# Attention backward: two passes over stored exponentials, or one pass with dS transposed by a DMA

## The chip, the cores and the metric

The kernel runs on one core of one Trainium2 chip. The metric is device time in microseconds (us) of one execution. The engines named below are PE (TensorE, matmuls), its weight loads (PEld), DVE (VectorE), ACT (ScalarE), POOL (GpSimd) and SP (SyncE, which only issues DMAs here).

## The reference

A transformer block, forward and backward (`jax.vjp`), with batch 1, S = 2048 tokens, D = 512, 32 heads of Dh = 16 columns and an MLP of F = 1792. The output and nine gradients are returned.

```python
def _A_ref(x, wqkv, wo):                       # H = 32, Dh = 16
    q, k, v = split heads of (x @ wqkv)
    scores = jnp.einsum('bhqd,bhkd->bhqk', q, k) * Dh ** (-0.5)
    p = _softmax(scores, axis=-1)
    o = jnp.einsum('bhqk,bhkd->bhqd', p, v)
    return merge heads of (o) @ wo
def _B_ref(x, w1, b1, w2, b2):
    r = relu(x @ w1 + b1)
    return (r * r) @ w2 + b2
mod = silu(c) @ w_mod          # sa, ca, ga, sb, cb, gb
x = x + ga * _A_ref(_layernorm(x) * (1 + ca) + sa, A_wqkv, A_wo)
x = x + gb * _B_ref(_layernorm(x) * (1 + cb) + sb, B_w1, B_b1, B_w2, B_b2)
_out, _vjp = jax.vjp(_f, ...); return (_out, *_vjp(grad_out))
```

For each head the attention backward needs P = exp(scale QK^T) (2048 x 2048), dP = dO V^T, dS = P * dP, and then dQ = dS K, dK = dS^T Q and dV = P^T dO. The 1/rowsum and the row term of the softmax gradient are folded into extra columns of the padded dO and V operands, so that dS is one product of two tiles.

## The kernel before

The work is cut in phases, which run one after the other: forward projections and attention (`phase12`), output projection and MLP forward (`phase3`), MLP backward and the gradient into the attention (`phase4`), attention backward (`phase5`), and the gradients of wqkv, wo and the modulation (`phase6`). Instructions are written in program order; a tile framework then sets buffers, semaphores and, by its own costs, some small moves in the order of each engine. Each engine executes its list in order.

**Units.** Attention is done for pairs of heads. For each of the 16 pairs (`pidx`, that is group `g` of four heads and half `jp`), each of four blocks of 512 columns (`c0`) and each of 16 blocks of 128 rows (`ib`) there is one unit: 1024 units in a pass. Heads are 16 columns wide, padded to 32 rows, so four heads fill the 128 rows of a transposed operand (`QTq_d`, `KTq_d`, `VTq_d`, `dOTq_d` in DRAM). A matmul over all 128 rows would mix the four heads, so one operand is a masked tile with zeros in the rows of the other three (`make_masked`, `load_masked`, L446 and L457).

**Forward** (L409 to L418): two score matmuls of 512 columns per unit, one exp of 1024 columns (ACT), eight matmuls of 17 columns with 128x128 pieces of `pu` as weights. With `self.stash` each `pu` is also stored to DRAM (`put_d`, L415, 256 KB per unit). The pool of `pu` has 8 buffers with `stash` and 3 without it.

**Pass A** (`attn_bwd_pass("A")`) makes dQ, with keys on the partitions. It loads `pu` back from `put_d` (L1185, on SP), makes dP with two matmuls of 512 columns (L1201), copies two of three dP tiles from PSUM with ACT (L1144), multiplies on DVE (L1145 from the copy, L1147 straight from PSUM), and adds eight matmuls of 16 columns into dQ (L1116). In it runs, as a background generator stepped every few units, the gradient of the MLP weights (`gen_4b_bg`, L805 to L885): 14 blocks of 128 MLP columns.

**Pass B** (`attn_bwd_pass("B")`) makes dK and dV, with queries on the partitions. Per unit it makes scores (L1190, two matmuls of 512 columns into `st`) and dP (L1193, two into `dp`), exp of the scores again (L1197, two of 512 columns), the product on DVE (L1147) and, two units late (`LAG`), sixteen matmuls of 16 columns: eight with `ds` as weights (L1120, dK), eight with `pu` as weights (L1123, dV). `st` has three PSUM buffers of one bank, `dp` two of two banks. At its start the loads for phase 6 (`wq_6`, `dx1b_6`, L1064 and L1065) are issued on POOL.

Of the kernel before, what the change touches and what calls it, by code (L numbers as in the profile page):

```python
# [33 lines left out]
class K:  # L34
# [29 lines left out]
    def build(self, ctx: ExitStack):  # L64
# [21 lines left out]
        self.stash = self.opts.get("stash", True)  # L86
# [963 lines left out]
    def phase45(self):  # L1050
        pass

    def phase5(self):
        tc, nc, pp, io = self.tc, self.nc, self.pp, self.io
        S, D, H, NQ, ST, DT = self.S, self.D, self.H, self.NQ, self.ST, self.DT
# [4 lines left out]
        self.dk_t = opb.tile([P, ST, D], BF16, name="dk_t")  # L1060
        self.dv_t = opb.tile([P, ST, D], BF16, name="dv_t")
# [6 lines left out]
    def attn_bwd_pass(self, mode, bg=None):  # L1068
        tc, nc = self.tc, self.nc
        S, D, H, NQ, ST = self.S, self.D, self.H, self.NQ, self.ST  # L1070
        loadA = (mode == "A" and self.stash)
        exp_split = self.opts.get("exp_split", False)
        LAG = self.opts.get("lagA", 3) if loadA else 2
        act_frac = self.opts.get("act_frac", (2, 3))
        with ExitStack() as es:
            cp = es.enter_context(tc.tile_pool(name=f"p5{mode}c", bufs=1))
            qp = es.enter_context(tc.tile_pool(name=f"p5{mode}q", bufs=2))
            sb = es.enter_context(tc.tile_pool(name=f"p5{mode}s", bufs=LAG + 2))
            bg_gen, bg_n = (None, 0)
            if bg is not None:  # L1080
                bg_gen, bg_n = bg(es)
            if loadA:
                ldp = es.enter_context(tc.tile_pool(name=f"p5{mode}ld", bufs=self.opts.get("ld_bufs", 15)))
                tmpp = es.enter_context(tc.tile_pool(name=f"p5{mode}tmp", bufs=3))
                dpp = es.enter_context(tc.tile_pool(name=f"p5{mode}dp", bufs=3, space=PSUM))
            else:
                stp = es.enter_context(tc.tile_pool(name=f"p5{mode}st", bufs=3, space=PSUM))
                dpp = es.enter_context(tc.tile_pool(name=f"p5{mode}dp", bufs=2, space=PSUM))
            accp = es.enter_context(tc.tile_pool(name=f"p5{mode}acc", bufs=1, space=PSUM))
            if mode == "A":  # L1090
                Ktm = cp.tile([P, ST, D], BF16, name="Ktm")
                nc.sync.dma_start(Ktm[:], self.ktm_d.rearrange("(st p) d -> p st d", p=P))
            else:
                Qtm = cp.tile([P, ST, D], BF16, name="Qtm")
                nc.sync.dma_start(Qtm[:], self.qtm_d.rearrange("(st p) d -> p st d", p=P))
                dOp = cp.tile([P, ST, D], BF16, name="dOp")
                nc.gpsimd.dma_start(dOp[:], self.dOp_d.rearrange("(st p) d -> p st d", p=P))
            accbank = accp.tile([P, 2, 256], F32, name="accbank")
            accbank4 = accbank[:].rearrange("p a (b c) -> p (a b) c", b=2)
            nacc = 128 if mode == "A" else 256  # L1100
            pend = []
            state = {"grp": 0, "u": 0}
            units_total = 2 * NQ * self.SC * ST
            bg_every = max(1, (units_total * 9 // 10) // max(1, bg_n))

            def stage4(u):
                (g, jp, c0, cw, ib, nib, heads, rows, acc, pu, ds) = u
                nsub = cw // P
                if ib == 0:
                    nc.vector.memset(acc[:, :nacc], 0.0)  # L1110
                for a in range(2):
                    h = heads[a]
                    for sub in range(nsub):
                        if mode == "A":
                            o = acc[:, (a * 4 + sub) * DH:(a * 4 + sub + 1) * DH]
                            nc.tensor.matmul(o, lhsT=ds[:, a, sub * P:(sub + 1) * P], rhs=Ktm[:, ib, h * DH:(h + 1) * DH],  # L1116
                                             start=False, stop=False, skip_group_check=True)
                        else:
                            o = acc[:, (a * 4 + sub) * DH:(a * 4 + sub + 1) * DH]
                            nc.tensor.matmul(o, lhsT=ds[:, a, sub * P:(sub + 1) * P], rhs=Qtm[:, ib, h * DH:(h + 1) * DH],  # L1120
                                             start=False, stop=False, skip_group_check=True)
                            o2 = acc[:, 128 + (a * 4 + sub) * DH:128 + (a * 4 + sub + 1) * DH]
                            nc.tensor.matmul(o2, lhsT=pu[:, a, sub * P:(sub + 1) * P], rhs=dOp[:, ib, h * DH:(h + 1) * DH],  # L1123
                                             start=False, stop=False, skip_group_check=True)
                if ib == nib - 1:
                    st0 = c0 // P
                    h0 = heads[0]
                    if mode == "A":
                        dst = self.dq_t[:, st0:st0 + nsub, h0 * DH:(h0 + 2) * DH].rearrange("p s (a d) -> p a s d", a=2)
                        src = acc[:, 0:128].rearrange("p (a s d) -> p a s d", a=2, s=4)[:, :, :nsub, :]  # L1130
                        nc.vector.tensor_scalar(dst, src, self.scale, None, ALU.mult)
                    else:
                        dst = self.dk_t[:, st0:st0 + nsub, h0 * DH:(h0 + 2) * DH].rearrange("p s (a d) -> p a s d", a=2)
                        src = acc[:, 0:128].rearrange("p (a s d) -> p a s d", a=2, s=4)[:, :, :nsub, :]
                        nc.vector.tensor_scalar(dst, src, self.scale, None, ALU.mult)
                        dst = self.dv_t[:, st0:st0 + nsub, h0 * DH:(h0 + 2) * DH].rearrange("p s (a d) -> p a s d", a=2)
                        src = acc[:, 128:256].rearrange("p (a s d) -> p a s d", a=2, s=4)[:, :, :nsub, :]
                        nc.scalar.copy(dst, src)

            def consumer(dp, pu, cw):  # L1140
                ds = sb.tile([P, 2, 512], BF16, name="ds")
# [337 lines left out]
```

The softmax here doesn't subtract the row's maximum and nothing guards it: scores larger than these inputs give would overflow.

## Time and profile before

| what | value |
|---|---|
| runs of the kernel | 3949.59 and 3952.64 us, median 3951.11 |
| span of the profiled execution | 3955.1 us |
| busy share PE / DVE / ACT / POOL | 87% / 68% / 77% / 8% |
| DMA | 727.01 MB, mean 184 GB/s |
| PE from / to: pass A (L1201, L1116) | 1474.8 to 2434.0 us |
| PE from / to: pass B (L1193, L1123) | 2439.8 to 3782.7 us |
| phase 6 (first matmul L1235) | from 3796.1 us |

The runs shown were taken without the profiler. The profiled execution is known by its span alone, 4 us (0.1%) above their median; sums in this text are made against 3955.1 and then lowered by 4. In the profile a share of busy time is an average over phases with different limits, so the phases are read one by one. A matmul's record lasts until its result is written; the next one starts earlier than that, so the distance between two starts is what a matmul costs when they follow each other.

### The profile page before, as it was taken

What the parts mean: (1) busy time and instruction counts of PE and PEld (TensorE: products, weight loads), DVE (VectorE), ACT (ScalarE), POOL (GpSimd) and SP (SyncE); (2) the same over time, 40 slices, a digit from 0 to 9 for tenths busy, and PEclk for the clock granted to TensorE, in tenths of its full rate; (3) what the DMA queues carried; (4) which work ended last, traced back from release to release, by engine and by line L of the source; (5) the groups of instructions that cost most, each with busy time, mean ns of one, the idle gap of its engine ahead of it and who ended that gap; (6) DMA issues with size and microseconds to landing.
All of it is one profiled execution on the core that took longest, in us unless ns stands there. A gap on an engine that the chain in (4) does not pass through costs nothing. (4 is left out here: it accounts for less than half of the span.)

```text
span 3955.1 us, 109981 instructions
## 1 busy us (share of the span) xinstructions
PE 3447.8 (87%) x44824; PEld 1950.4 (49%) x45590; DVE 2683.9 (68%) x3839; ACT 3053.2 (77%) x4423; POOL 334.0 (8%) x428
## 2 busy tenths in 40 slices
PE   5999988888686848888888878999999999999987
PEld 2555533333233325555555544666666666666643
DVE  6222210000244649999999998999999999999965
ACT  3999999999532438888888767888888888888843
POOL 3111100000100340111111110000000000000000
PEclk8999999999898969999999999999999999999998
DMA  3999988887724679999999897000000000000032
GB/s 123 333 333 336 332 309 292 298 297 289 263 91 163 212 190 332 322 320 337 321 322 329 289 323 231 9 18 9 19 20 8 19 9 18 19 9 6 2 125 74
DMA packets 414007, 727.01 MB, mean 184 GB/s; under 512 B 52697, under 2 KB 121050, under 8 KB 413498
## 3 DMA queue, kind: packets, MB, share of 16 engines
q1 hardware_dynamic: 381114, 630.90, 45.9%
q0 software_dynamic: 23760, 79.32, 5.9%
q10 hardware_dynamic: 8624, 9.70, 0.8%
q8 instruction: 356, 5.83, 0.6%
q14 instruction: 153, 1.25, 0.1%
HBM read 383.65 MB, written 336.07 MB: 182 GB/s over the span
## 5 line engine op out<-in xcount | busy, mean ns | idle before, releaser
L1147 DVE TENSOR_TENSOR ds<-dp,pu 128x1024 bf16<-128x1024 f32 x1365 | 1658.4, 1220 | 71.6 <-ACT pu L1197 24.0
L1197 ACT ACTIVATE pu<-st 128x512 bf16<-128x512 f32 x2048 | 1112.6, 597 | 229.9 <-PE st L1190 167.2
L412 ACT ACTIVATE pu<-st 128x1024 bf16<-128x1024 f32 x1024 | 938.8, 1621 | 0.0
L1144 ACT CAST dpb<-dp 128x1024 bf16<-128x1024 f32 x683 | 666.3, 1026 | 180.5 <-PE dp L1201 149.1
L1201 PE MATMUL dp<-dOTm,VTq 128*128 128x512 bf16 x1853 | 567.0, 382 | 96.7 <-ACT dpb L1144 78.2
L1190 PE MATMUL st<-KTm,QTq 128*128 128x512 bf16 x2047 | 628.0, 378 | 23.9 <-ACT pu L1197 16.6
L409 PE MATMUL st<-QTm,KTq 128*128 128x512 bf16 x1856 | 564.8, 377 | 9.6 <-ACT pu L412 4.4
L1120 PEld LDWEIGHTS <-ds 128*128 128x128 bf16 x8192 | 499.6, 96 | 115.0 <-DVE ds L1147 0.9
L1193 PE MATMUL dp<-VTm,dOTq 128*128 128x512 bf16 x1729 | 540.0, 379 | 5.5 <-DMA KTm<-KTq_d 5.5
L1120 PE MATMUL accbank<-Qtm,ds 128*128 128x16 bf16 x8192 | 529.1, 170 | 17.4 <-DVE ds L1147 0.7
L1123 PE MATMUL accbank<-dOp,pu 128*128 128x16 bf16 x8192 | 525.7, 169 | 0.0
L1123 PEld LDWEIGHTS <-pu 128*128 128x128 bf16 x8192 | 458.1, 96 | 113.6 <-issue 0.3
L1145 DVE TENSOR_TENSOR ds<-dpb,pu 128x1024 bf16<-128x1024 bf16 x683 | 472.8, 708 | 58.0 <-ACT dpb L1144 54.5
L418 PEld LDWEIGHTS <-pu 128*128 128x128 bf16 x8192 | 293.5, 96 | 443.3 <-ACT pu L412 381.2
L1116 PEld LDWEIGHTS <-ds 128*128 128x128 bf16 x8192 | 318.5, 96 | 247.5 <-DVE ds L1145 59.1
L418 PE MATMUL accbank<-Vaug,pu 128*128 128x17 bf16 x8192 | 352.3, 172 | 91.2 <-ACT pu L412 41.1
L427 DVE RECIPROCAL rl<-accbank 128x4 f32<-128x4 f32 x128 | 22.9, 179 | 527.4 <-PE accbank L418 527.3
L1116 PE MATMUL accbank<-Ktm,ds 128*128 128x16 bf16 x8192 | 336.7, 170 | 21.8 <-DVE ds L1145 6.0
L1193 PEld LDWEIGHTS <-dOTq 128*128 128x128 bf16 x2048 | 196.8, 96 | 287.0 <-DVE ds L1147 34.6
L1201 PEld LDWEIGHTS <-VTq 128*128 128x128 bf16 x2048 | 159.9, 96 | 162.2 <-issue 116.7
L288 DVE TENSOR_SCALAR ev_fm<-pps,bcol 128x512 bf16<-128x512 f32 x92 | 69.1, 751 | 186.4 <-PE pps L281 184.3
L409 PEld LDWEIGHTS <-KTq 128*128 128x128 bf16 x2048 | 130.4, 96 | 40.9 <-issue 24.2
(308 smaller groups left out, 2676.5 us busy)
## 6 DMA issues: line engine op xcount, KB each, us to landing
put_d<-pu SPq DMA_DIRECT2D x1024, 256.0 KB
pu<-put_d SPq DMA_DIRECT2D x1024, 256.0 KB
rT_d<-rT SPq DMA_DIRECT2D x4, 1792.0 KB
rT<-rT_d SPq DMA_DIRECT2D x4, 1792.0 KB
duT_d<-duT POOLq DMA_DIRECT2D x4, 1792.0 KB, 12.8
rT_f<-rT_d POOLq DMA_DIRECT2D x14, 512.0 KB, 6.6
duT_f<-duT_d POOLq DMA_DIRECT2D x14, 512.0 KB, 7.2
xhat_d<-xhat SPq DMA_DIRECT2D x2, 2048.0 KB
```

The source lines that it names most:

```text
L409: nc.tensor.matmul(stt[:, a, :qw], lhsT=KT[:, kb * P:(kb + 1) * P], rhs=QTm[a][:, q0:q0 + qw], start=True, stop=True)
L412: nc.scalar.activation(pu[:, :, :qw], stt[:, :, :qw], ACT.Exp, scale=self.scale)
L418: nc.tensor.matmul(acc[:, a, sub, :], lhsT=pu[:, a, sub * P:(sub + 1) * P], rhs=Vaug[:, kb, heads[a], :], start=False, stop=False, skip_gr ...
L1116: nc.tensor.matmul(o, lhsT=ds[:, a, sub * P:(sub + 1) * P], rhs=Ktm[:, ib, h * DH:(h + 1) * DH], start=False, stop=False, skip_group_check ...
L1120: nc.tensor.matmul(o, lhsT=ds[:, a, sub * P:(sub + 1) * P], rhs=Qtm[:, ib, h * DH:(h + 1) * DH], start=False, stop=False, skip_group_check ...
L1123: nc.tensor.matmul(o2, lhsT=pu[:, a, sub * P:(sub + 1) * P], rhs=dOp[:, ib, h * DH:(h + 1) * DH], start=False, stop=False, skip_group_chec ...
L1144: nc.scalar.copy(tmp[:, :, :cw], dp[:, :, :cw])
L1147: nc.vector.tensor_tensor(ds[:, :, :cw], dp[:, :, :cw], pu[:, :, :cw], ALU.mult)
L1190: nc.tensor.matmul(sts[a][:, :cw], lhsT=L1[:, ib * P:(ib + 1) * P], rhs=R1[a][:, c0:c0 + cw], start=True, stop=True)
L1193: nc.tensor.matmul(dp[:, a, :cw], lhsT=L2[:, ib * P:(ib + 1) * P], rhs=R2[a][:, c0:c0 + cw], start=True, stop=True)
L1197: nc.scalar.activation(pu[:, a, :cw], sts[a][:, :cw], ACT.Exp, scale=self.scale)
L1201: nc.tensor.matmul(dp[:, a, :cw], lhsT=L2[:, ib * P:(ib + 1) * P], rhs=R2[a][:, c0:c0 + cw], start=True, stop=True)
```

## The change

`self.stash` is set to False: the forward pass stores no `pu`, and its pool has 3 buffers. The MLP weight gradients leave the background of pass A and run by themselves before the attention backward (`phase45`, with `gen_4b` in place of `gen_4b_bg`). The two passes become one, `attn_bwd`, with queries on the partitions as in pass B. Its score and dP matmuls take 32 rows of both operands, without masked tiles. dK and dV are made as in pass B (`kv`, two units late). For dQ, the `ds` tiles of two units, 128 x 2048 values or 512 KB, are transposed in sixteen 128x128 blocks by one DMA on SP's queue (`dma_start_transpose`, L1177), and three pairs late (`LAGQ`) sixteen matmuls of 16 columns with the transposed blocks as weights add into dQ (`dq`, L1137). `st` has two PSUM buffers, one for each head. All loads of operands go through POOL's queue, one group of four heads ahead; the loads for phase 6 come after the pass. The lines that the diff removes are those of `phase5` and `attn_bwd_pass` above.

```diff
-        self.stash = self.opts.get("stash", True)
+        self.stash = False
...
     def phase45(self):
-        pass
+        with tc.tile_pool(name="p4b", bufs=1) as sb2, tc.tile_pool(name="p4bl", bufs=2) as lb, \
+                tc.tile_pool(name="p4bo", bufs=2) as ob, \
+                tc.tile_pool(name="p4bacc", bufs=1, space=PSUM) as accps, \
+                tc.tile_pool(name="p4bps", bufs=2, space=PSUM) as ps, \
+                tc.tile_pool(name="p4btr", bufs=1, space=PSUM) as trps:
+            for _ in self.gen_4b(sb2, lb, ob, accps, ps, trps):
+                pass
     def phase5(self):
-        self.attn_bwd_pass("A", bg=self.bg_4b)
+        self.attn_bwd()
         opb = self.open_pool("p56b", bufs=1)
...
         nc.gpsimd.dma_start(self.wq_6[:], io["A_wqkv"].rearrange("(kt p) n -> p kt n", p=P))
         nc.gpsimd.dma_start(self.dx1b_6[:], self.dx1b_d.rearrange("(st p) d -> p st d", p=P))
-        self.attn_bwd_pass("B")
...
+    def attn_bwd(self):
+        LAG, LAGQ = 2, 3
+        W = 4 * DH
+            qp = es.enter_context(tc.tile_pool(name="p5q", bufs=2))
+            pup = es.enter_context(tc.tile_pool(name="p5pu", bufs=LAG + 3))
+            dsp = es.enter_context(tc.tile_pool(name="p5ds", bufs=5))
+            dtp = es.enter_context(tc.tile_pool(name="p5dt", bufs=LAGQ + 2))
+            stp = es.enter_context(tc.tile_pool(name="p5st", bufs=2, space=PSUM))
+            dpp = es.enter_context(tc.tile_pool(name="p5dp", bufs=2, space=PSUM))
+            accp = es.enter_context(tc.tile_pool(name="p5acc", bufs=1, space=PSUM))
+            acckv = accp.tile([P, 2, 2, 2, 4, DH], F32, name="acckv")
+            accq = accp.tile([P, ST, 2, DH], F32, name="accq")
...
+            def kv(u):
...
+                    for sub in range(4):
+                        nc.tensor.matmul(acc[:, 0, a, sub, :], lhsT=ds[:, a, sub * P:(sub + 1) * P],
+                                         rhs=T["Q"][:, ib, col:col + DH], start=False, stop=False, skip_group_check=True)
+                        nc.tensor.matmul(acc[:, 1, a, sub, :], lhsT=pu[:, a, sub * P:(sub + 1) * P],
+                                         rhs=T["dO"][:, ib, col:col + DH], start=False, stop=False, skip_group_check=True)
...
+            def dq(u):
...
+                for i in range(2):
+                    for a in range(2):
+                        for sub in range(4):
+                            nc.tensor.matmul(accq[:, ib0 + i, a, :], lhsT=dsT[:, (i * 2 + a) * 4 + sub, :],
+                                             rhs=T["K"][:, 4 * c + sub, col:col + DH], start=False, stop=False,
+                                             skip_group_check=True)
...
+                        for ib0 in range(0, ST, 2):
+                            ds2 = dsp.tile([P, 2, 2, 512], BF16, name="ds")
+                            for i in range(2):
+                                sts = [stp.tile([P, 512], F32, name="st") for a in range(2)]
+                                dp = dpp.tile([P, 2, 512], F32, name="dp")
+                                for a in range(2):
+                                    r = 32 * (2 * jp + a)
+                                    nc.tensor.matmul(sts[a][:], lhsT=T["QT"][r:r + 32, q], rhs=T["KT"][r:r + 32, c0:c0 + 512],
+                                                     start=True, stop=True)
+                                for a in range(2):
+                                    r = 32 * ((2 * jp + a + 2) % 4)
+                                    nc.tensor.matmul(dp[:, a, :], lhsT=T["dOT"][r:r + 32, q], rhs=T["VT"][r:r + 32, c0:c0 + 512],
+                                                     start=True, stop=True)
+                                pu = pup.tile([P, 2, 512], BF16, name="pu")
+                                for a in range(2):
+                                    nc.scalar.activation(pu[:, a, :], sts[a][:], ACT.Exp, scale=self.scale)
+                                if len(pend) >= LAG:
+                                    kv(pend.pop(0))
+                                nc.vector.tensor_tensor(ds2[:, i], dp[:], pu[:], ALU.mult)
+                                pend.append((T, g, jp, c, ib, acc, pu, ds2[:, i]))
+                            dsT = dtp.tile([P, 16, P], BF16, name="dsT")
+                            nc.sync.dma_start_transpose(dsT[:], ds2[:].rearrange("p i a k -> p (i a k)"))
+                            if len(pendq) >= LAGQ:
+                                dq(pendq.pop(0))
+                            pendq.append((T, g, jp, c, ib0, dsT))
```

What `gen_4b` does for each of its 14 blocks `ft` (line numbers of the kernel after the change):

```python
nc.scalar.activation(aT_f[:], rT_f[:], ACT.Square)
for (srcT, dst, eng) in ((aT_f, a_blk, "act"), (duT_f, du_blk, "dve")):
    for s0 in range(0, ST, 8):                        # two groups of eight
        pt = trps.tile([P, 8 * P], BF16, name="trps") # one PSUM buffer
        ...                                           # 8 transposes (L717), one copy out by eng
g2 = ...   # 16 matmuls of 512 columns (L725), then two DVE products and an f32 matmul (L731)
g4 = ...   # 64 matmuls of 128 columns (L736), an f32 matmul (L741), six DVE operations
```

**One unit on PE, before (pass B).** `st` and `dp` are the tiles of scores and dP, `KTm` and `VTm` the masked operands; each large matmul covers 128 rows.

```order
L1190 LDWEIGHTS QTq_60875
L1190 MATMUL st_61797<-KTm0_39029,QTq_60875 128x512
L1190 LDWEIGHTS QTq_60875
L1190 MATMUL st_61798<-KTm1_39031,QTq_60875 128x512
L1193 LDWEIGHTS dOTq_60877
L1193 MATMUL dp_61771<-VTm0_39037,dOTq_60877 128x512
L1193 LDWEIGHTS dOTq_60877
L1193 MATMUL dp_61771<-VTm1_39039,dOTq_60877 128x512
L1120 LDWEIGHTS ds_61739
L1120 MATMUL accbank_39028<-Qtm_39024,ds_61739 128x16
L1123 LDWEIGHTS pu_61720
L1123 MATMUL accbank_39028<-dOp_39026,pu_61720 128x16
```

The same place in PE's list after the change, with the end of a `dq` (`dsT` is the transposed tile, `Kg` the group's K):

```order
L1137 LDWEIGHTS dsT_28071
L1137 MATMUL accq_20930<-Kg_20953,dsT_28071 128x16
L1163 LDWEIGHTS QTq_20945
L1163 MATMUL st_28311<-KTq_20947,QTq_20945 128x512
L1163 LDWEIGHTS QTq_20945
L1163 MATMUL st_28312<-KTq_20947,QTq_20945 128x512
L1137 LDWEIGHTS dsT_28144
L1137 MATMUL accq_20930<-Kg_20953,dsT_28144 128x16
```

The four large matmuls stay; they now take unmasked operands at 32 rows each, and the small matmuls of `dq` stand in the same list, here even between `st` and `dp`. In most units (878 of 1024) the four stand together; PE's list goes from one kind of matmul to the other 2449 times in all.

**SP's queue, before (pass A).** The loads of stored exponentials alternate with those of masked operands.

```order
L457 DMA dOTm_19712<-dOTq_d 32x512
L1185 DMA pu<-put_d 128x1024 x3
L457 DMA dOTm_19714<-dOTq_d 32x512
L1185 DMA pu<-put_d 128x1024 x12
L457 DMA dOTm_19712<-dOTq_d 32x512
```

After the change SP has the transposes alone between the stores of `gen_4b` (L728, L751) and the first DMAs of phase 6:

```order
L728 DMA out_dram<-dw_20763 128x512
L751 DMA out_dram<-dw_20843 128x4x128
L1177 DMA_TRANSPOSE dsT<-ds 128x16x128 x512
L1365 DMA out_dram<-dwm_59021 128x4x512
L1199 DMA O_tm<-O_d 128x16x512
```

The 1024 loads of 256 KB, and in the forward pass as many stores, have left; 512 transposes of 512 KB have come, and whatever follows them on SP starts after the last of them is issued.

More of the change, by code (lines that the diff above doesn't have):

```diff
@@ L1109, in stage4 @@
                 if ib == 0:
-                    nc.vector.memset(acc[:, :nacc], 0.0)
+                    nc.vector.memset(acc, 0.0)
                 for a in range(2):
[L1112 to L1138, printed above, removed]
@@ new lines, in kv @@
+                    col = (2 * jp + a) * DH
+                    for sub in range(4):
[3 more added lines that the diff above has]
+                                         rhs=T["dO"][:, ib, col:col + DH], start=False, stop=False, skip_group_check=True)
@@ new lines, in attn_bwd @@
+            T = load_group(0)
+            n = 0
+            for g in range(NQ):
+                Tn = load_group(g + 1) if g + 1 < NQ else None
+                for jp in range(2):
+                    for c in range(SC):
+                        c0 = 512 * c
+                        acc = acckv[:, n % 2]
+                        n += 1
+                        for ib0 in range(0, ST, 2):
+                            ds2 = dsp.tile([P, 2, 2, 512], BF16, name="ds")
+                            for i in range(2):
+                                ib = ib0 + i
+                                q = slice(ib * P, (ib + 1) * P)
+                                sts = [stp.tile([P, 512], F32, name="st") for a in range(2)]
[20 more added lines that the diff above has]
+                            pendq.append((T, g, jp, c, ib0, dsT))
+                T = Tn
@@ L1210, in attn_bwd_pass @@
             while pend:
-                stage4(pend.pop(0))
-            if bg_gen is not None:
-                for _ in bg_gen:
-                    pass
+                kv(pend.pop(0))
+            while pendq:
+                dq(pendq.pop(0))
     def phase6(self):
```

147 lines of the change are left out of this document (36 added, 111 removed).

## The prediction

> **What bounds the kernel now.** I read the page's first line, then the busy time of each engine in five stretches cut where the phases begin (forward; MLP and preparation; pass A; pass B; phase 6), because one share for the whole span mixes stages with different limits.
>
> ```profile
> span 3955.1 us, 109981 instructions
> ```
>
> ```profile
> core 0: us, PE busy (x) PEld busy (x) DVE busy (x) ACT busy (x) POOL busy (x), PEclk, DMA share, GB/s
> 90.00:1050.00 960.00, 836.53 (x10574) 404.86 (x10768) 157.35 (x504) 942.76 (x1027) 66.87 (x122) 0.99 0.85 311
> 1050.00:1474.00 424.00, 291.90 (x1541) 139.82 (x1569) 207.07 (x475) 143.36 (x282) 97.96 (x118) 0.84 0.52 165
> 1474.00:2436.00 962.00, 835.30 (x11612) 511.69 (x11818) 893.15 (x1229) 762.55 (x869) 130.85 (x140) 0.98 0.93 317
> 2436.00:3786.00 1350.00, 1304.88 (x20175) 810.40 (x20497) 1271.53 (x1157) 1115.51 (x2112) 6.55 (x11) 1.00 0.06 17
> 3786.00:3956.00 170.00, 132.11 (x724) 62.77 (x736) 96.71 (x266) 60.64 (x99) 3.16 (x5) 0.90 0.35 112
> ```
>
> The forward stretch is ACT's (942.76 of 960). Pass A has DVE (893) and DMA (0.93) both near their end; pass B has PE (1305) and DVE (1272) near theirs, with almost no DMA. The change replaces 962 + 1350 = 2312 us by one pass and a foreground phase. Which engine is really full in pass B is seen in its timeline, one unit of it:
>
> ```profile
> 3000.34 0.59 PE L1190 MATMUL st<-KTm,QTq 128*128 128x512 bf16 x2
> 3000.76 1.08 ACT L1197 ACTIVATE pu<-st 128x512 bf16<-128x512 f32 x2 [0.18 <-PE st L1190]
> 3000.78 0.59 PE L1193 MATMUL dp<-VTm,dOTq 128*128 128x512 bf16 x2
> ...
> 3001.20 0.17 PE L1120 MATMUL accbank<-Qtm,ds 128*128 128x16 bf16 x1
> ...
> 3001.23 0.17 PE L1123 MATMUL accbank<-dOp,pu 128*128 128x16 bf16 x1
> ...
> 3001.59 0.17 PE L1123 MATMUL accbank<-dOp,pu 128*128 128x16 bf16 x1
> ...
> 3001.61 0.59 PE L1190 MATMUL st<-KTm,QTq 128*128 128x512 bf16 x2
> ```
>
> From one unit's first score matmul to the next is 3001.61 - 3000.34 = 1.27 us without a hole: four large matmuls at (3001.20 - 3000.34)/4 = 0.216, sixteen small ones at (3001.61 - 3001.20)/16 = 0.0255. PE bounds pass B, ACT waits for it, and DVE is close behind, as its group and the wait show (mean ns of one before the last bar):
>
> ```profile
> L1147 DVE TENSOR_TENSOR ds<-dp,pu 128x1024 bf16<-128x1024 f32 x1365 | 1658.4, 1220 | 71.6 <-ACT pu L1197 24.0
> L1197 ACT ACTIVATE pu<-st 128x512 bf16<-128x512 f32 x2048 | 1112.6, 597 | 229.9 <-PE st L1190 167.2
> L1190 PE MATMUL st<-KTm,QTq 128*128 128x512 bf16 x2047 | 628.0, 378 | 23.9 <-ACT pu L1197 16.6
> L1120 PE MATMUL accbank<-Qtm,ds 128*128 128x16 bf16 x8192 | 529.1, 170 | 17.4 <-DVE ds L1147 0.7
> ```
>
> ```profile
> ACT pu L1197 <- PE st L1190: 137.2, 683, 0.5
> ```
>
> **The new pass.** Per unit DVE keeps its 1.22 us and ACT its 2 x 0.597 = 1.19. PE gets 24 small matmuls in place of 16 (0.61 us). The four large ones are unknown twice over. They use four different sets of 32 rows, so they may run side by side: from 0.216 apart (as now) down to nothing; I take a quarter, 0.054. And where the list passes from small to large matmuls PE may have to finish what it holds: 0.170 - 0.025 = 0.15 behind a small one and 0.378 - 0.216 = 0.16 behind a large one by the records' lengths, or nothing. I take both in full, as the careful end: an overlap of two shapes is in no row. What these two choices are worth depends on a loop, since `st` has one buffer per head where it had three in common. From the end of a unit's second exp: 0.04 until PE takes the next unit's second score matmul (3000.76 lies 0.04 after the first one's 0.38), then dP, dP at 0.054 each and 0.38 to the end of the last: 0.53; 16 `kv` at 0.0255 and, in every other unit, 16 `dq`: 0.82; finish, 0.15; the following unit's first score, 0.38 + 0.04; its two exps, 1.19. That is 3.11 us, in which two units pass: 512 x 3.11 = 1592. I take **1590**. With no price for the passing the large ones need 0.04 + 3 x 0.054 before `kv`, and the loop is 0.20 + 0.82 + 0.42 + 1.19 = 2.63 (DVE alone 2.44): 512 x 2.63 = 1347, and with the 64 column ends, at which `acckv` is cleared and written out by DVE, about 1390, the lower bound.
>
> ```profile
> L1135 DVE TENSOR_SCALAR dk_t<-accbank 128x128 bf16<-128x128 f32 x64 | 18.6, 291 | 10.5 <-PE accbank L1123 10.4
> L1138 ACT CAST dv_t<-accbank 128x128 bf16<-128x128 f32 x64 | 16.7, 260 | 3.0 <-DVE dk_t L1135 3.0
> L1110 DVE MEMSET accbank<- 128x256 f32 x53 | 14.4, 272 | 2.7
> ```
>
> (64 x (0.29 + 0.26 + 0.27) = 52 us.) With nothing side by side and both prices, PE alone needs per two units 8 x 0.216 + 48 x 0.0255 + 2 x 0.31 = 3.57: 1828, the upper bound.
>
> [...]
>
> **The transposes.** No row shows one. 512 of them, of 512 KB, must each be through the queue in 3.11 us to be hidden. `dq` comes three pairs late, so latency is covered by about two pairs, 6 us; the rate counts. From below, pass A's plain loads, 317 GB/s at a DMA share of 0.93: 524288 B / 317 = 1.65 us. From above, if each 256-byte piece (one row of a 128x128 block, 2048 in a transpose) takes a packet as ACT's queue shows them, 0.008 x 16 x 3955.1 / 8624 = 59 ns, over 16 engines: 7.5 us.
>
> ```profile
> q10 hardware_dynamic: 8624, 9.70, 0.8%
> ...
> pu<-put_d SPq DMA_DIRECT2D x1024, 256.0 KB
> ...
> dOTq<-dOTq_d POOLq DMA_DIRECT2D x8, 512.0 KB, 5.1
> ...
> dx1b<-dx1b_d POOLq DMA_DIRECT2D x1, 2048.0 KB, 19.2
> ...
> wqkv<-in_A_wqkv_dram POOLq DMA_DIRECT2D x1, 1536.0 KB, 10.2
> ```
>
> I take 1.65: same queue, nearly the same rows per partition (2 KB there, 4 KB here), and at the time of the pass hardly any other DMA. At that, nothing of it is on the path. If it isn't so, the weight load of L1137 waits on PE, behind it stand the next units' scores, and ACT and DVE run dry.
>
> [...]
>
> **The MLP gradients in the foreground.** Rows of the background version and of an f32 matmul:
>
> ```profile
> 1979.97 0.61 PE L834 MATMUL gps<-ident,rT_f 128*128 128x128 bf16 x8
> ```
>
> ```profile
> 1967.35 1.11 PE L851 MATMUL gps<-du_blk,xh 128*128 128x128 bf16 x17
> ```
>
> ```profile
> 1478.25 1.56 PE L808 MATMUL gps<-g2w,ones_f 128*128 128x512 f32 x2
> ```
>
> ```profile
> L835 ACT COPY a_blk<-gps 128x1024 bf16<-128x1024 bf16 x28 | 28.8, 1028 | 1.1 <-PE gps L834 1.0
> L826 ACT ACTIVATE rT_f<-rT_f 128x2048 bf16<-128x2048 bf16 x14 | 27.3, 1948 | 0.0
> ```
>
> A 128-column matmul costs (1.11 - 0.22)/16 = 0.056 us (0.22 is one record's length). Per block PE has (32 + 64) x 0.056 + 16 x 0.216 + about 1.0 in f32 = 9.9 us. One PSUM buffer takes all four groups of transposes, so two ACT copies (1.03) and part of the DVE copies stand in the way: about 2.6 more, 12.5 us, times 14 = 175, and 15 for the start and the closing sums: **190**. Bounds: 140 (PE alone, 14 x 9.9) and 240 (copies and the square, 1.95, all in line: 14 x 17).
>
> **The rest.** The first group's seven loads are at the pass's start (5.1 us for one of 512 KB): 20, from 5 to 40. The last transpose and `dq`: 8, from 4 to 12. Phase 6's loads come late now (19.2 us to landing), where pass B covered them: 10, from 0 to 20. The masked loads had cover already. In the forward pass the stores go, which leaves ACT's chain as it is:
>
> ```profile
> L412 ACT ACTIVATE pu<-st 128x1024 bf16<-128x1024 f32 x1024 | 938.8, 1621 | 0.0
> ```
>
> ACT has no idle time ahead of this exp: 0. Either sign is possible: up to 17 us gained (960 - 943), or as much lost if three `pu` buffers hold up the exp; its cover is that PE uses `pu` at once.
>
> **Sum**, on the profiled span: 1474 + 190 + 20 + 1590 + 8 + 10 + 170 = 3462. The span is 4 above the median of the runs: **3460**, 12% less than before.
>
> **Rivals.**
> - *The shapes mix freely* (pass 1390): 3262 - 4 = 3258. For it: the rows are disjoint. Against: list order and the one `st` buffer per head.
> - *The transposes set the pace, below break-even.* A transpose of 3.6 us, the middle between 3.1 and 4.07, makes the pass 512 x 3.6 = 1843 and the time 3711. For it: one queue issues all, in order, and no row shows how fast it issues pieces of this kind. Against: 3.1 us is only 524288 B / 3.1 us = 169 GB/s, where plain loads made 317. [...]
> - *The transposes are slow, and the kernel is slower than before.* The other terms sum to 1872, so it decides from (3955 - 1872)/512 = 4.07 us on. At 5.0 us the pass is 2560 and the time 4428; at the upper bound of 7.5, 5708. For it: if the transpose goes in pieces of 256 bytes at the pace of the packet row, it takes 7.5. Against: the source rows are 4 KB long, and pass B's DMA share of 0.06 says that the engines are free.
> - *The change doesn't do what it says*: the 32-row matmuls follow one another, with both prices. Pass 1828, time 3696; still faster, and in the forecast's own range.
>
> **How the numbers follow.** Forecast 0.44 (own range 3340 to 3700, with the 240 of the foreground's end), free mixing 0.12, pace below break-even 0.15, slow transposes 0.29. The kernel's runs can tell 2% from no change: faster means below 3872, slower above 4030. Faster is 0.44 + 0.12 + 0.15 less 0.02 near the edge: 0.69; within 2% 0.04; slower 0.27. The range starts at 3220 (free mixing with a cheap foreground, 0.02 left out) and reaches to 4450, transposes of 5.0 us; beyond that I leave 0.17.
>
> **What would show it.** In the changed kernel's profile: distance between units in the middle of the pass (1.55 forecast; 1.3 for free mixing); starts of the four large matmuls (0.05 or 0.22 apart); idle PE before the first small one. If the transposes set the pace, PE's weight load of L1137 waits for a DMA and the pass is 512 times the distance of two transposes. The foreground should lie between 1474 and some 1665. The forecast is wrong first of all if a transpose takes over 3.1 us.

## The result and the profile after

| what | before | after |
|---|---|---|
| median of the runs | 3951.11 us | 3645.28 us (3640.79 to 3649.78) |
| span of the profiled execution | 3955.1 us | 3638.7 us |
| attention backward (first to last PE instruction) | 1474.8 to 3782.7 | 1644.2 to 3463.7 |
| mean granted PE clock | 0.97 | 0.72 |

The time falls to 0.9226 of before (0.9198 to 0.9254): 7.7% less, where 12% was forecast. The first rows of the page and of its picture of the span:

```profile
span 3638.7 us, 99498 instructions
...
PEclk8999999999989897995555555555555555555588
DMA  3111100000032555639999999999999999999952
```

The clock row reads 5 from slice 19 to slice 38 of 40: over the new pass, and in no other slice, PE is granted half its clock. The stretches, cut as before (forward; MLP and preparation; the foreground of MLP gradients; the pass; phase 6):

```profile
core 0: us, PE busy (x) PEld busy (x) DVE busy (x) ACT busy (x) POOL busy (x), PEclk, DMA share, GB/s
90.00:1050.00 960.00, 840.84 (x10564) 400.45 (x10762) 157.14 (x501) 942.18 (x1026) 65.71 (x119) 0.99 0.09 29
1050.00:1460.00 410.00, 286.34 (x1525) 137.59 (x1551) 197.45 (x479) 143.11 (x281) 84.78 (x105) 0.85 0.50 161
1460.00:1643.00 183.00, 154.43 (x1625) 108.57 (x1640) 96.14 (x182) 58.59 (x57) 17.74 (x32) 0.97 0.46 145
1643.00:3466.00 1823.00, 1675.89 (x28679) 954.96 (x28681) 1309.12 (x1252) 1120.45 (x2051) 44.00 (x54) 0.50 0.94 162
3466.00:3640.00 174.00, 133.05 (x732) 63.04 (x744) 95.96 (x261) 58.71 (x96) 4.05 (x7) 0.90 0.37 123
```

The two passes' 2312 us have become 183 + 1823. The forward stretch lost all its stores (DMA share 0.85 to 0.09) and got no shorter (942.18 us of ACT's work after 942.76). In the pass PE is the fullest engine (1676 of 1823), at half clock, and the DMA engines are nearly as full (0.94). Three units of PE's timeline, and ACT's rows of the same place:

```profile
2499.07 0.61 PE L1163 MATMUL st<-KTq,QTq 32*128 32x512 bf16 x2
2499.08 0.61 PE L1167 MATMUL dp<-VTq,dOTq 32*128 32x512 bf16 x2
2499.62 0.19 PE L1118 MATMUL acckv<-Qg,ds 128*128 128x16 bf16 x1
...
2500.36 1.07 PE L1163 MATMUL st<-KTq,QTq 32*128 32x512 bf16 x2
2500.86 0.61 PE L1167 MATMUL dp<-VTq,dOTq 32*128 32x512 bf16 x2
2501.40 0.19 PE L1118 MATMUL acckv<-Qg,ds 128*128 128x16 bf16 x1
...
2501.84 0.57 PE L1137 MATMUL accq<-Kg,dsT 128*128 128x16 bf16 x16
2502.35 0.61 PE L1163 MATMUL st<-KTq,QTq 32*128 32x512 bf16 x2
2502.36 0.61 PE L1167 MATMUL dp<-VTq,dOTq 32*128 32x512 bf16 x2
```

```profile
2499.71 1.08 ACT L1171 ACTIVATE pu<-st 128x512 bf16<-128x512 f32 x2 [0.92 <-PE dp L1167]
2500.98 1.09 ACT L1171 ACTIVATE pu<-st 128x512 bf16<-128x512 f32 x2 [0.18 <-PE st L1163]
2502.99 1.09 ACT L1171 ACTIVATE pu<-st 128x512 bf16<-128x512 f32 x2 [0.92 <-PE dp L1167]
```

The four large matmuls start together (2502.35 and 2502.36 for both pairs) and are through 0.54 later (2499.08 to 2499.62): they do run side by side, but one record is about 0.60 where before it was 0.38. (In the unit between, at 2500.36, the first score goes some 0.49 ahead of the other three, which wait for the second `st` buffer.) The pair of units lasts 2502.99 - 2499.71 = 3.28 us, and the loop of the forecast can be read off: exps until 2500.79, second `dp` at 2500.86 (0.07), first `kv` at 2501.40 (0.54), `dq` at 2501.84 (0.44), next `st` at 2502.35 (0.51), exp at 2502.99 (0.64), two exps 1.08. The whole pass, from the first score matmul to the last `dq`, takes 1819.5 us or 1819.5/512 = 3.55 per pair (groups by line: ns min/median/max, first and last start):

```profile
L1163 PE MATMUL st<-KTq,QTq x2048: 577/602/604, 1644.2 to 3455.4; 32*128 32x512 bf16 x187
```

```profile
L1137 PE MATMUL accq<-Kg,dsT x8192: 174/174/221, 1666.1 to 3463.7; 128*128 128x16 bf16 x200
```

The waits in the pass (1700 to 3400 us: us in total, times, longest) show where some of the rest is:

```profile
ACT pu L1171 <- PE dp L1167: 392.8, 392, 12.5
...
PEld L1137 <- DMA dsT<-ds: 83.4, 44, 12.2
...
PE accq L1137 <- DMA dsT<-ds: 62.1, 18, 11.7
```

PE's weight loads wait 83 us for transposes and its matmuls 62 us, in few pieces, some of them 12 us long. These are mostly the same stalls, seen once at a weight load and once at the matmul behind it (12.2 and 11.7), so the two sums overlap, and the 145 us that one of the expectations below makes of them counts a stall twice (as do the 307 us of another, at 128 rows). So two things were on trial: **theory C**, the half clock makes the pass long, and **theory T**, the transposes do.

### The profile page after: what moved, and what is told of

Read it like the earlier page. It is cut to its first block, busy times and chain, and to the rows that moved or that the text cites. A ratio compares the mean times of both kernels' runs of the same rounds, so it can differ in the third digit from the quotient of the medians.

```text
span 3638.7 us, 99498 instructions
## 1 busy us (share of the span) xinstructions
PE 3137.8 (86%) x43331; PEld 1685.7 (46%) x43588; DVE 1912.1 (53%) x2886; ACT 2351.3 (65%) x3545; POOL 245.9 (7%) x351
## 2 busy tenths in 40 slices
DMA packets 1180482, 449.39 MB, mean 124 GB/s; under 512 B 1093514, under 2 KB 1149452, under 8 KB 1180044
## 5 line engine op out<-in xcount | busy, mean ns | idle before, releaser
L1174 DVE TENSOR_TENSOR ds<-dp,pu 128x1024 bf16<-128x1024 f32 x1024 | 1251.8, 1224 | 508.5 <-ACT pu L1171 364.3
L1163 PE MATMUL st<-KTq,QTq 32*128 32x512 bf16 x2048 | 844.9, 594 | 81.4 <-ACT pu L1171 31.1
L1118 PEld LDWEIGHTS <-ds 128*128 128x128 bf16 x8192 | 485.0, 104 | 418.9 <-issue 418.7
L1167 PE MATMUL dp<-VTq,dOTq 32*128 32x512 bf16 x2048 | 621.9, 603 | 2.4 <-DMA VTq<-VTq_d 2.3
L1118 PE MATMUL acckv<-Qg,ds 128*128 128x16 bf16 x8192 | 573.1, 176 | 0.5 <-DMA Qg<-qtm_d 0.4
L1120 PE MATMUL acckv<-dOg,pu 128*128 128x16 bf16 x8192 | 554.4, 174 | 0.4 <-DMA dOg<-dOp_d 0.4
L1137 PE MATMUL accq<-Kg,dsT 128*128 128x16 bf16 x8192 | 329.1, 175 | 69.5 <-DMA dsT<-ds 69.2
L1137 PEld LDWEIGHTS <-dsT 128*128 128x128 bf16 x8192 | 273.8, 104 | 223.3 <-issue 130.5
L1163 PEld LDWEIGHTS <-QTq 32*128 32x128 bf16 x2048 | 137.2, 99 | 69.0 <-issue 10.0
L281 PE MATMUL pps<-xhat1T,wpad 128*128 128x512 bf16 x372 | 119.9, 378 | 7.8 <-DVE ev_fm L288 3.8
```

The lines of the kernel that those rows point to most:

```text
L281: nc.tensor.matmul(pt[:, :sw], lhsT=wpads[t][:, kt, g, :], rhs=xhat1T[:, kt, s0:s0 + sw], start=(kt == 0), stop=(kt == DT - 1))
L1118: nc.tensor.matmul(acc[:, 0, a, sub, :], lhsT=ds[:, a, sub * P:(sub + 1) * P], rhs=T["Q"][:, ib, col:col + DH], start=False, stop=False, s ...
L1120: nc.tensor.matmul(acc[:, 1, a, sub, :], lhsT=pu[:, a, sub * P:(sub + 1) * P], rhs=T["dO"][:, ib, col:col + DH], start=False, stop=False, ...
L1137: nc.tensor.matmul(accq[:, ib0 + i, a, :], lhsT=dsT[:, (i * 2 + a) * 4 + sub, :], rhs=T["K"][:, 4 * c + sub, col:col + DH], start=False, s ...
L1163: nc.tensor.matmul(sts[a][:], lhsT=T["QT"][r:r + 32, q], rhs=T["KT"][r:r + 32, c0:c0 + 512], start=True, stop=True)
L1167: nc.tensor.matmul(dp[:, a, :], lhsT=T["dOT"][r:r + 32, q], rhs=T["VT"][r:r + 32, c0:c0 + 512], start=True, stop=True)
```

## The experiments

The pass is measured from the first score matmul to the last `dq`. Kernels timed with an interval are compared with the kernel before; a time without an interval is that of a single run.

### 1. No transposes

```diff
-dsT = dtp.tile([P, 16, P], BF16, name="dsT")
-nc.sync.dma_start_transpose(dsT[:], ds2[:].rearrange("p i a k -> p (i a k)"))
+dsT = ds2                                   # dq takes ds2's blocks; ds has 10 buffers
```

> The pass of the changed kernel lasts 1823 us (1643 to 3466), 3.56 us for two units, with a granted clock of 0.50 and a DMA share of 0.94. This kernel issues no transposes; dq takes the untransposed blocks of ds as weights (dQ is another sum), so PE's list is the same. Theory C (clock: the 32-row matmuls are what halves the clock, and the loop over PE and ACT at half clock sets the pace): clock still 0.50; the loop by the trace is 0.04 + 0.53 + 0.86 + 0.08 + 0.65 + 1.09 = 3.25 us, so the pass is 1660 to 1700 and the span about 3500. Theory T (transposes: 2048 pieces of 256 bytes each fill the DMA engines, PE starves, and its clock falls because it starves): clock about 1.0, pass 1400 to 1600, span 3220 to 3420.

Its windows view, over the middle of the pass:

```profile
1700.00:3300.00 1600.00, 1531.06 (x26287) 873.46 (x26284) 1199.17 (x1146) 1025.46 (x1879) 33.67 (x42) 0.50 0.05 13
```

3572.76 us; pass 1649.3 to 3396.4 = 1747. DMA share 0.05 instead of 0.94, clock still 0.50, and only 72 us gained. The transposes are neither what takes the clock down nor the greater part of the loss. 1747 is above what either theory asked for: at 3.41 per pair the loop read above (3.28, 1679 in all) accounts for it but for 68 us. They stand where a column of 512 (eight pairs) ends, that is where DVE writes `dk_t` and `dv_t` and clears `acckv`. ACT's first exps in the first, second and third pair of one column:

```profile
2195.62 1.08 ACT L1171 ACTIVATE pu<-st 128x512 bf16<-128x512 f32 x2 [0.92 <-PE dp L1167]
...
2198.89 1.08 ACT L1171 ACTIVATE pu<-st 128x512 bf16<-128x512 f32 x2 [0.92 <-PE dp L1167]
...
2203.34 1.09 ACT L1171 ACTIVATE pu<-st 128x512 bf16<-128x512 f32 x2 [1.61 <-PE st L1163]
```

The first pair takes 2198.89 - 2195.62 = 3.27 us, the second 2203.34 - 2198.89 = 4.45, and that is the median over the columns too: 64 x 1.18 = 76 us, a little of which the third pair gives back. The forecast put the column ends at 52.

### 2. One `dq` matmul of 16

```diff
-                        for sub in range(4):
+                        for sub in (range(1) if (i, a) == (0, 0) else ()):
```

> All transposes, but one of the sixteen matmuls of each dq (dQ is incomplete), which still waits for the transposed tile. PE's loop is shorter by 15 x 0.0267 = 0.40 us for two units. If the transposes have a floor of their own under the pace (theory T), it stays near 3.4 to 3.5 us for two units, pass 1740 to 1800, DMA share 0.95 or more. If only the loop at half clock counts (theory C), it falls to about 2.85 + 0.28 us of waits, pass 1600, DMA share above 0.94 only if the engines can go faster.

3479.32 us; pass 1656.5, or 3.24 per pair with every transpose still there: between what the two theories asked for. So the queue passes a transpose in 3.24 us or less, and 163 us of the 15 x 512 x 0.0267 = 205 that left PE came off the end: PE's list is still the main limit, though not the only one.

### 3. 128 rows, in the new pass

```diff
-fm = {"QT": self.QTq_d, "KT": self.KTq_d, "dOT": self.dOTq_d, "VT": self.VTq_d}
+fm = {"QT": self.QTq_d, "dOT": self.dOTq_d}
+masked = self.make_masked(cp, ["KT", "VT"])   # loaded on POOL, one pair of heads ahead
...
-nc.tensor.matmul(sts[a][:], lhsT=T["QT"][r:r + 32, q], rhs=T["KT"][r:r + 32, c0:c0 + 512],
+nc.tensor.matmul(sts[a][:], lhsT=T["QT"][:, q], rhs=masked["KT"][2 * jp + a][:, c0:c0 + 512],
```

(`dp` in the same way.)

> The changed kernel with masked operands of 128 rows for scores and dP, as pass B had them; the transposes stay. Theory C: clock back to 0.97 to 1.00. PE alone then needs 8 x 0.216 + 48 x 0.0255 = 2.95 us for two units, so the pass is 1590 if the transposes have no floor, 1720 to 1760 if their 0.94 x 3.56 = 3.35 us is one; span 3410 to 3580. Theory T: clock still about 0.5 to 0.6, and with large matmuls one after another at half clock (0.43 each) the pass is 2000 or more, span above 3800.

Its windows view, and its group of score matmuls (ns min/median/max):

```profile
1700.00:3300.00 1600.00, 1435.15 (x26137) 944.16 (x26592) 1205.26 (x1160) 1033.53 (x1900) 55.52 (x86) 0.95 1.07 169
```

```profile
L1175 PE MATMUL st<-KTm,QTq x2048: 376/376/634, 1646.3 to 3364.7; 128*128 128x512 bf16 x187
```

The clock is back (0.95) beside the same transposes, a large matmul is 376 ns again, and the pass takes 1726 although nothing runs side by side any more: 3552.98 us, 0.8986 of before (0.8971 to 0.9001). The 32 rows made the new kernel slower by 94 us of pass.

### 4. 32 rows, in the old pass B

```diff
-srcs = {"QT": self.QTq_d, "dOT": self.dOTq_d}
-msrcs = {"KT": (self.KTq_d, 0), "VT": (self.VTq_d, 2)}
+srcs = {"QT": self.QTq_d, "dOT": self.dOTq_d, "KT": self.KTq_d, "VT": self.VTq_d}
+msrcs = {}
...                                            # matmuls on [r:r + 32] of both operands
```

> The kernel before, with pass B's scores and dP on 32-row operands without masks (three st buffers, no transposes, pass A untouched). Theory C: the granted clock of pass B falls from 1.00 to about 0.50; a unit on PE then takes about 0.08 + 0.53 + 0.43 = 1.04 us, so DVE sets the pace at 1.25 to 1.30 and the span stays at 3900 to 3970. Theory T: clock of pass B stays at 1.00, with the same DVE pace, span 3890 to 3920.

The middle of pass B in the kernel before, and then in this one (windows view):

```profile
2500.00:3700.00 1200.00, 1163.55 (x18070) 724.04 (x18356) 1137.21 (x1032) 999.11 (x1892) 3.19 (x6) 1.00 0.05 13
```

```profile
2500.00:3700.00 1200.00, 1179.85 (x19013) 629.61 (x19010) 1145.83 (x1071) 1031.36 (x1962) 6.35 (x12) 0.50 0.04 13
```

No transpose and no DMA to speak of, PE busy 0.98 of the time, and the clock goes from 1.00 to 0.50 with this edit alone. The time is 3895.12 us, 1.5% below the 3953.97 beside it, in a single run: in pass B, where PE had no hole at full clock, four large matmuls side by side at half clock (0.54 us where all four start together) still cost less than four in line at full clock (4 x 0.216 = 0.86).

### 5. 128 rows and no transposes

Experiments 1 and 3 together.

> Masked operands of 128 rows and no transposes (dq takes the untransposed blocks of ds, so dQ is another sum): both suspects gone. With 128 rows the granted clock was 0.95 and the pass 1722 us; with 32 rows and no transposes it was 0.50 and 1747. If the two costs are separate (half clock alone is worth what is left without transposes, waits for transposes what is left at full clock), this pass is PE's: 8 x 0.216 + 48 x 0.0255 = 2.95 us for two units and some waiting at the two st buffers, 3.0 to 3.15, so 1540 to 1620 us, span 3370 to 3450, clock 0.97 or more. If the pass stays above 1700, something else that all these kernels share (two st buffers, order of the list) sets the pace and not the clock or the DMA.

```profile
1700.00:3100.00 1400.00, 1374.51 (x25641) 926.41 (x26092) 1177.73 (x1135) 1013.81 (x1865) 55.52 (x86) 1.00 0.06 16
```

3361.61 us, pass 1541, clock 1.00 in the windows view. With it the four corners of the two theories (pass, us) are complete:

| | transposes | none | they cost |
|---|---|---|---|
| 32 rows (clock 0.50) | 1819.5 | 1747 | 72 |
| 128 rows (0.95, 1.00) | 1726 | 1541 | 185 |
| the 32 rows cost | 94 | 206 | |

Without transposes the 32 rows cost 206 us, though they run four at a time; with them a part of the slower pace is cover for the transposes, so the two costs do not add.

### 6. Each transpose twice

```diff
+dsT2 = dtp.tile([P, 16, P], BF16, name="dsT2")
+nc.sync.dma_start_transpose(dsT2[:], ds2[:].rearrange("p i a k -> p (i a k)"))
```

> The changed kernel with every transpose issued twice, the second into a tile that nothing reads. It prices one transpose on the DMA engines, F: the pace becomes the larger of 3.56 us and 2F for two units. If F is what one transpose took in the pass with one dq matmul (1650 us / 512 = 3.2 us with a DMA share of 1.03), the pass is about 3280 us and the span about 5090. If the engines had room (F of 1.65 us, as for plain loads), the pass stays at 1820 to 1900 us.

Its windows view and its group of `dq` matmuls:

```profile
1700.00:4400.00 2700.00, 1979.90 (x27098) 968.36 (x27096) 1200.47 (x1178) 1062.49 (x1940) 33.72 (x42) 0.50 1.16 196
```

```profile
L1137 PE MATMUL accq<-Kg,dsT x8192: 172/174/197, 1672.0 to 4521.9; 128*128 128x16 bf16 x200
```

Here the queue sets the pace: 2872 us for 1024 transposes, **2.80 us each** (524288 B / 2.80 = 187 GB/s), PE busy only 1980 of 2700. (A DMA share over 1, here 1.16, means that the packets' times, summed, overlap.) Neither of the two numbers expected (3.2 and 1.65) came out, and 2.80 is still below the 3.41 to 3.55 per pair that the pass took. What in the queue is slow is open: SP's two issue records last 2.36 and 2.64 us at the median, 4.99 of the 5.61 us of a pair, so the issuing and the moving of the data were not told apart.

### 7. A longer lag

```diff
-LAG, LAGQ = 2, 3
+LAG, LAGQ = 2, 6                            # ds 6 buffers, dsT 8
```

> The changed kernel with dq six pairs late in place of three, and 8 dsT and 6 ds buffers. If PE's 145 us of waits for transposed tiles come from single late ones (one stall of 10 to 14 us where a group's loads of 128-byte pieces share the DMA engines, and small ones between), most of them go: pass 1823 to about 1740, as without transposes (1747), span 3550 to 3580. If they come from the rate of the engines, they stay: pass 1800 or more, span 3620 to 3640.

The same two waits in this kernel (1700 to 3200 us):

```profile
PEld L1137 <- DMA dsT<-ds: 8.8, 7, 2.1
...
PE accq L1137 <- DMA dsT<-ds: 6.8, 6, 1.6
```

The 83 and 62 us of waits become 9 and 7, and the pass 1764: close to the 1747 without transposes. What the transposes cost in the new kernel was lateness, not rate. (The sixth `ds` buffer is not what did it: in the kernel after, DVE has no wait for a transpose.) In the kernel after, the longest wait comes where a group of heads begins:

```profile
1874.23 1.17 POOL L1107 DMA_DIRECT2D Qg<-qtm_d  x1 [2.09 <-PE accq L1137]
1875.40 1.16 POOL L1107 DMA_DIRECT2D dOg<-dOp_d  x1
...
1891.38 0.30 PE L1137 MATMUL accq<-Kg,dsT 128*128 128x16 bf16 x5 [11.72 <-DMA dsT<-ds]
```

The loads of Q and dO, in pieces of 128 bytes, are issued some 16 us earlier. PE's trace has one such hole, of 7.1 to 11.7 us, behind each of the seven issues of a group's loads, 62 us in all. So the loads beside them are read as what makes single transposes late, and `dq` three pairs late is then not late enough. This is argued from the place; experiment 8 supports it.

### 8. 128 rows, Q and dO resident

```diff
+R[n_] = rp.tile([P, ST, D], BF16, name=f"{n_}r")     # n_ in ("Q", "dO"), loaded once, 1 KB rows
+nc.gpsimd.dma_start(R[n_][:], tm.pop(n_).rearrange("(st p) d -> p st d", p=P))
```

> Masked 128-row operands as in the kernel with full rows, and token-major Q and dO loaded once in rows of 1 KB instead of per group in 128-byte pieces (K stays per group). With full rows PE waited for transposed tiles for 307 us in 1600 (171 at weight loads, 136 at matmuls), of which some 20 to 35 us at each of the group changes. If the group loads are what delays the transposes, the pass falls from 1722 to 1630 to 1670 and the span from 3550 to 3460 to 3500. If the rate of the transposes alone sets the pace (3.2 us or more for two units), it stays at 1690 to 1720.

3489.04 us, 0.8823 (0.8808 to 0.8838), pass 1662. Two thirds of a group's small pieces are gone, and 64 us with them, which supports the reading of experiment 7; `dq` still waits for transposes:

```profile
PEld L1151 <- DMA dsT<-ds: 114.4, 74, 5.1
...
PE accq L1151 <- DMA dsT<-ds: 79.6, 63, 4.6
```

The longest is 5.1 us, against 11.6 in experiment 3.

### 9. 128 rows and the longer lag

Experiment 3 with experiment 7's numbers.

> Masked 128-row operands and dq six pairs late (8 dsT, 6 ds buffers); transposes kept. A transpose costs the DMA engines 2.80 us by the run with two of each (1024 in 2872 us), less than the 3.01 us for two units that PE took at full clock without transposes (1541 us). If lateness and not the rate is what is left at full clock, the pass falls from 1726 to 1560 to 1620 and the span from 3550 to 3380 to 3450, faster than with Q and dO resident (3489). If the rate with the group loads beside it is the bound, it stays at 1660 or more.

```profile
1700.00:3100.00 1400.00, 1332.90 (x24609) 892.23 (x25038) 1133.57 (x1091) 972.29 (x1790) 55.67 (x86) 0.99 1.19 183
```

3437.43 us, **0.8708 of before (0.8689 to 0.8727)**: the best version run here, 208 us below the change as made. Pass 1606, 3.14 per pair: 120 of the 185 us that the transposes cost at 128 rows went with the longer lag. PE (busy 1333 of 1400 us) and the transposes (DMA share 1.19; it was 1.16 in experiment 6, where the queue was the limit at 2.80) are now both near their end; which of them would bind next was not tried.

### 10. Which matmuls, and how many rows

Both are experiment 3 with one edit: scores alone on 32 rows, dP on 128; and scores on 64 rows beside dP on the other 64.

```diff
-lhsT=T["QT"][:, q], rhs=masked["KT"][2 * jp + a][:, c0:c0 + 512]
+lhsT=T["QT"][r:r + 32, q], rhs=masked["KT"][2 * jp + a][r:r + 32, c0:c0 + 512]
```

> Scores on 32 rows, dP on masked 128 rows, otherwise as the kernel with full rows (clock 0.95, pass 1726). If the granted clock follows how many rows of the array the large matmuls fill, it lies between 0.50 and 0.95 on the mean of the pass, or alternates. If any 32-row matmul in the loop is enough, it is 0.50 and the pass about 2000 (dP at 0.43 us each, one after another: 0.86 us more per unit than side by side). If the clock follows only how long PE is busy, it stays at 0.95 and the pass at 1700 to 1750.

```diff
-lhsT=T["QT"][:, q], rhs=masked["KT"][2 * jp + a][:, c0:c0 + 512]
+lhsT=T["QT"][64 * jp:64 * jp + 64, q], rhs=masked["KT"][2 * jp + a][64 * jp:64 * jp + 64, c0:c0 + 512]
```

> Scores on 64 rows (two heads, one of them zero in the masked operand) and dP on the other 64, otherwise as the kernel with full rows. Half of the array's rows per large matmul, and scores and dP of one unit can run side by side. If the clock follows the rows filled over time, 64 rows side by side with 64 keep it near 0.95 and the pass is at the transposes' waits, 1700 to 1750, or shorter. If it follows the height of a single matmul, it falls to 0.50 as with 32 rows, and the pass is 1800 to 1950.

Windows views of the first and of the second:

```profile
1700.00:3700.00 2000.00, 1887.26 (x25130) 1026.94 (x25570) 1171.14 (x1113) 996.87 (x1826) 55.49 (x86) 0.50 0.72 131
```

```profile
1700.00:3600.00 1900.00, 1847.49 (x26174) 872.64 (x26172) 1197.84 (x1137) 1021.27 (x1871) 55.51 (x86) 0.50 0.79 141
```

Both at 0.50: half of the large matmuls on 32 rows are enough, and so are 64 rows. The first run's dP, on all 128 rows, shows that a record grows with the clock and not with the rows: 607 ns at the median, against 376 at clock 1.00.

```profile
L1179 PE MATMUL dp<-VTm,dOTq x1553: 587/607/634, 1650.0 to 3889.4; 128*128 128x512 bf16 x195
```

The times are 4076.41 us (pass 2249) and 3912.27 us (pass 2085), both longer than expected. The second's size I had wrong, and its timeline shows at least a part of the reason:

```profile
2502.90 0.60 PE L1175 MATMUL st<-KTm,QTq 64*128 64x512 bf16 x1
2502.91 0.60 PE L1179 MATMUL dp<-VTm,dOTq 64*128 64x512 bf16 x1
2503.30 0.63 PE L1175 MATMUL st<-KTm,QTq 64*128 64x512 bf16 x1
```

A score and a dP start together, the next two 0.40 later: two at a time instead of four, at the same low clock.

## Why the prediction was right, and where it missed

The direction held, and 3645 lies inside the forecast's own range; against the sum of 3462 the profiled span, 3638.7, is 177 us over. By its own terms, forecast and measured: start of the pass 1474 + 190 + 20 = 1684, measured 1644 (40 less); pass 1590, measured 1819.5 (230 more); tail and phase 6 188, measured 3638.7 - 3463.7 = 175 (13 less). **The pass is the term that was mis-sized**, by three parts: the loop 512 x (3.28 - 3.11) = 87 us, the column ends about 70, late transposes about 72.

*The loop.* Its shape was right: ACT waits for PE in every pair, as listed, and the rival of free mixing (1390; its terms, 1347 and 52, sum to 1399) fell: the first `kv` starts 0.54 us after the four large ones, not 0.20 as that rival had it. Forecast 3.11 and read 3.28, part by part: `dp` until the first `kv` 0.61 against 0.53; 32 small matmuls 0.44 + 0.43 against 0.82; passing to the large ones 0.08 against 0.15; the first score until its exp 0.64 against 0.42; two exps 1.08 against 1.19 (the timeline shown with the prediction already had 1.08). So the step that failed in the loop is "0.38": the length of a large matmul was carried over from rows at clock 1.00, and 32 rows brought the clock to 0.50 (experiments 3 and 4), where a record is 0.60 (experiment 10 shows it for 128 rows too). I had asked what 32 rows do to the distance of four matmuls and not whether they change the duration of each. The side-by-side guess (0.054 apart) was cautious, the price of a change of shape and the exps too dear, and all three hid part of the clock's cost: that the loop came out only 0.17 off is luck. So is it that the pass stayed under the upper bound of 1828, which was worked out for four matmuls in line at full clock; they ran side by side at half clock.

*The column ends* (52) were worked out for the lower bound and left out of the central 1592 without a reason; experiment 1 shows about 70 us there, 1.18 in the second pair of a column.

*The transposes.* 1.65 was wrong, and the transposes do go in pieces of 256 bytes, as the upper bound took them; that the pieces are the reason was not shown. Packets in experiment 1, which has no transposes, and in the kernel after:

```profile
DMA packets 115513, 180.81 MB, mean 51 GB/s; under 512 B 28554, under 2 KB 84492, under 8 KB 115084
```

```profile
DMA packets 1180482, 449.39 MB, mean 124 GB/s; under 512 B 1093514, under 2 KB 1149452, under 8 KB 1180044
```

(1093514 - 28554)/512 = 2080 each: the 2048 rows of a transpose's blocks and 32 more. They move 449.39 - 180.81 = 268.58 MB, 252 bytes a packet on the mean. But a piece does not cost what the row of the other queue said: 2.80 us, not 7.5. That is under the pace, so "nothing of it is on the path" held for the rate, by less than was thought: 2.80 against 3.11, where 1.65 was forecast. It did not hold for "latency is covered by about two pairs": single ones keep PE waiting up to 12 us, which is worth 72 us of pass (experiments 1 and 7).

*The rivals on the transposes.* The pace below break-even (3711) came close in the time and is not the cause: without any transpose the pass keeps 1747 of its 1819.5. Its point that one queue issues all, at a pace in no row, did not decide either: SP issued two per 5.6 us in experiment 6, and in the kernel after it was waiting for DVE:

```profile
L1177 SPq DMA_TRANSPOSE dsT<-ds x512: 1669/2078/10077, 1651.4 to 3457.9; - x171
```

```profile
SPq L1177 <- DVE ds L1174: 1085.3, 457, 22.4
```

An issue's record is 2.08 us at the median. The slower kernel (from 4.07 us per transpose on) did not come.

*The rest.* Foreground with its loads 210 forecast, 183 in its stretch; the stretch ahead of it took 410 us where it had taken 424. Forward 0 forecast, and ACT's busy time there is 942.18 after 942.76. Both were argued from an engine's busy time in one stretch, and both came near.

## What to carry to other kernels

Carry a duration over only with the clock at which it was taken: where a change alters the shape of the matmuls, ask what it does to the granted clock, and price the rest at both 1.00 and 0.50. Matmuls on part of the rows paid in pass B (1.5%, in a single run) and lost in the new pass (94 to 206 us). PE was full with matmuls in line in both (in the new pass 1374.51 of 1400 us in experiment 5), but in the new pass ACT waits for the end of a score in every pair, so a longer matmul stands in the loop. That the single `st` buffer per head makes the difference was not tried. A transfer that is fast enough on average still needs a lag that covers its latest one: three more pairs of lag were worth 116 us here (3552.98 to 3437.43), for three more buffers of `dsT` and one of `ds`.

## What the runs showed of the hardware

- **Large matmuls on 32 or 64 rows held PE's granted clock at 0.50** in eight kernels (the kernel after, experiments 1, 2, 4, 6 and 7, both of 10), with PE busy up to 0.98 of the stretch; on 128 rows it was 0.95 to 1.00 (experiments 3, 5, 8 and 9). Being busy by the records was not enough for the full clock: 0.98 of the stretch in experiment 4 went with 0.50. What sets the granted clock was not tried further: a list with 32-row matmuls and more 128-row work could show it.
- At half clock a 512-column matmul's record is 0.602 us on 32 rows and 0.607 on 128, instead of 0.376, while 16-column ones follow each other at 0.0267 instead of 0.0255: here the clock hit the long matmuls almost alone.
- Four 32-row matmuls on different rows start within some 0.01 us (2502.35 and 2502.36 in the kernel after). Passing from 128 to 32 rows costs some 0.08 us more than the next small matmul would (the last small one starts at 2501.84 + 0.57 - 0.17 = 2502.24, the next `st` 0.11 later, against 0.027). The score starts 0.06 us before the record of the last small one ends (2502.41), so it did not wait for that record's end.
- A DMA transpose of 512 KB between tiles of SBUF took 2.80 us when its queue was the limit (experiment 6), 187 GB/s, in 2080 packets under 512 B.
